# A fused attention and two MLPs on one core: the second MLP's first product by Strassen's algorithm, its second in blocks of 512 columns

## Chip, cores and metric

The kernel runs on one core of one Trainium2 chip. The metric is the device time of one execution in microseconds; the median of three runs of the kernel before is 1016.05 us (1014.8 to 1016.28).

## What is computed

Linear attention with an exponential feature map over 4 batches of 8 heads, 576 tokens each, is followed by two MLPs on the 2304 tokens (512 features, 2048 hidden). The change touches the last one only.

```python
def _moe_ref(x, w_in, w_out):          # first MLP
    h = x @ w_in                       # [2304, 512] @ [512, 2048]
    g = h * (1.0 / (1.0 + np.exp(-h)))
    return (g @ w_out).astype(np.float32)

def _moe2_ref(x, w_in, w_out):         # second MLP
    h = np.maximum(x @ w_in, 0.0)
    return (h * h @ w_out).astype(np.float32)
...
    x = _moe_ref(x=x, **moe_kwargs)
    return _moe2_ref(x=x, **moe2_kwargs)
```

## The kernel before

All data lie transposed: features on the 128 partitions, tokens in the columns. Nearly every float32 factor is split into a high part (ACT casts it, `hi_act`, L351) and a low part (DVE subtracts, `lo_on`, L355), and one product of 128 x 128 weights with a block of tokens is three matmuls: low weights by high tokens, high by low, high by high.

The hidden features are 16 chunks of 128. `chunk(L, i, c, key)` does MLP `L`, token block `i`, chunk `c`: `gemm1` (L987) is 4 parts of 128 input features by three matmuls, 12 matmuls into one PSUM bank `h`; ACT and DVE make the gate out of it (L993, L1000 in the first MLP; relu on ACT, L995, and a multiply on DVE, L1004, in the second), ACT and DVE split the gated block into `gh` and `gl` (L351, L355), and `gemm2` (L1032) adds it with 12 matmuls to the four banks `o` of the output features. The first MLP takes 8 blocks of 288 tokens, the second 6 blocks of 384. After chunk 15 the four banks are evacuated by ACT (L1057) and DVE (L1059) and stored (L1062), the first MLP's to `x2d` in DRAM, from which `x2_of` loads and splits the second MLP's input (L1085).

The second MLP's weights are converted from 64-bit numbers during the attention and the first MLP (`w_conv`, four DVE operations of each 128 x 512 piece, L477 to L487), stored to `w2d` in DRAM (L541), and loaded again and split (`w2_load`, L561, and `w_split`) when the first MLP's weights leave their buffers.

The order is set by a planner (`Plan`): each operation has a key (its due time in units of one chunk), an engine and an assumed cost; `Plan.run` plays the program through and writes each engine's instructions in the order in which they came up. On the chip each engine works that list in order and waits by semaphores.

Of the kernel before, what the change touches and what calls it, by code (L numbers as in the profile page):

```python
# [279 lines left out]
def attention_then_two_mlps(ctx, tc, kT, qT, v, w_phi, w1, w2, out):  # L280
# [264 lines left out]
    stage, staged = [], []  # L545

    def stage_slot():
        if not stage:
            for k in range(2):
                t = wide_pool().tile([128, 3, 512], F32, tag=f"x{k}", name=f"stage{k}")  # L550
                stage.extend(t[:, i] for i in range(3))
        staged.append(stage[len(staged) % len(stage)])
        return staged[-1]

    def w2_load(c, part, key):
        k = ("wf", 1, c, part)
# [640 lines left out]
```

## Time and profile before

| | before |
|---|---|
| median of the runs | 1016.05 us |
| the profiled execution | 1015.75 us |
| its span, first to last instruction | 1013.6 us |
| TensorE (PE) busy | 998.1 us, 98% |
| VectorE (DVE) busy | 603.7 us, 60% |
| ScalarE (ACT) busy | 540.1 us, 53% |
| GpSimd (POOL) busy | 77.2 us, 8% |
| TensorE clock granted, mean | 0.993 |
| DMA, mean | 88 GB/s |

The span holds the instructions; 2.15 us of the execution lie around it. Attention and first MLP share the stretch to some 610 us, the second MLP has the rest. Matmul records overlap, since matmuls are pipelined: how fast they run is read from start to start, in the chain of waits or in the number of records in a window, and not from the mean duration of one.

### The profile page before, as it was taken

Reading aid. Unit: us, or ns where it says so; the run is one execution under the profiler, and the core shown is the slowest. Engines: PE = TensorE matmul, PEld = TensorE weight load, DVE = VectorE, ACT = ScalarE, POOL = GpSimd, SP = SyncE. Lnnn points to the kernel's source line nnn. Section 1 sums busy time; section 2 is a strip of 40 time slices with the busy share of each in tenths; the row PEclk is TensorE's granted clock in tenths of the full one; section 3 lists DMA queues with packets and bytes.
Section 4 is the critical chain, followed back from the end, with each engine's and each line's share of the span. In section 5 each row is a group of like instructions: output and inputs, shape, how many; then the busy total and the mean of one; then the engine's idle time right before and its main releaser. Section 6 shows DMA issues by size and latency. Waiting matters only on the chain.

```text
span 1013.6 us, 17252 instructions
## 1 busy us (share of the span) xinstructions
PE 998.1 (98%) x6656; PEld 971.9 (96%) x6656; DVE 603.7 (60%) x1137; ACT 540.1 (53%) x1295; POOL 77.2 (8%) x56
## 2 busy tenths in 40 slices
PE   9969999999999999999999999999999999999998
PEld 6739999999999999999999999999999999999998
DVE  5989997765656876888986786232232232322322
ACT  6867866776777776877753564232232222322222
POOL 3140003210012200021110000000000000000000
PEclk9979999999999999999999999999999999999999
DMA  8536601131112232544555864010010010100000
GB/s 263 183 112 213 216 25 39 58 86 49 38 32 58 66 113 79 183 131 141 148 137 170 288 219 140 14 51 14 1 63 1 8 55 1 48 1 1 32 1 32
DMA packets 46940, 88.88 MB, mean 88 GB/s; under 512 B 12426, under 2 KB 22794, under 8 KB 44810
## 3 DMA queue, kind: packets, MB, share of 16 engines
q1 hardware_dynamic: 46858, 87.78, 27.6%
q8 instruction: 52, 0.85, 0.3%
q14 instruction: 30, 0.25, 0.1%
HBM read 69.76 MB, written 17.92 MB: 86 GB/s over the span
## 4 chain that ended last, share of the span: by engine, by line
PE 96%; DVE 3%; issue 0%; ACT 0%; POOL 0%
PE h L987 40%; PE o L1032 40%; PE pn L911 5%; PE pk L652 3%; PE pkv L714 3%; PE pkv L760 3%; DVE w L355 1%; PE pq L848 1%; PE pq L849 1%; DVE wc L487 0%; PE pq L846 0%; POOL qm L859 0%; PE warm L439 0%; DVE wc L483 0%; DVE wc L477 0%
## 5 line engine op out<-in xcount | busy, mean ns | idle before, releaser
L1032 PE MATMUL o<-gh,w 128*128 128x288 f32 (+1 forms) x1792 | 442.8, 313 | 0.0
L1032 PEld LDWEIGHTS o<-gh,w 128*128 128x128 f32 x1792 | 313.0, 188 | 2.8 <-issue 2.1
L1032 PE MATMUL o<-gl,w 128*128 128x288 f32 (+1 forms) x896 | 278.7, 311 | 0.0
L987 PE MATMUL h<-x,w 128*128 128x288 f32 x1536 | 224.8, 295 | 0.1
L987 PE MATMUL h<-xw,w 128*128 128x384 f32 x1152 | 215.0, 334 | 0.0
L987 PEld LDWEIGHTS h<-x,w 128*128 128x128 f32 x1536 | 210.9, 188 | 1.0 <-ACT mx L674 0.4
L987 PEld LDWEIGHTS h<-xw,w 128*128 128x128 f32 x1152 | 201.0, 188 | 0.0
L1004 DVE TENSOR_TENSOR a<-h,a 128x384 f32<-128x384 f32 x96 | 53.5, 558 | 216.2 <-ACT a L995 216.0
L995 ACT ACTIVATE a<-h 128x384 f32<-128x384 f32 x96 | 47.2, 492 | 227.9 <-PE h L987 227.9
L1032 PEld LDWEIGHTS o<-gl,w 128*128 128x128 f32 x896 | 168.4, 188 | 0.2
L355 DVE TENSOR_TENSOR gl<-a,gh 128x288 fp32r<-128x288 f32 (+1 forms) x224 | 115.1, 514 | 63.6 <-ACT gh L351 61.3
L351 ACT CAST gh<-a 128x288 fp32r<-128x288 f32 (+1 forms) x224 | 105.3, 470 | 73.3 <-DVE a L1004 54.9
L859 POOL PARTITION_ALL_REDUCE qm<-qp x32 | 73.9, 2326 | 262.1 <-ACT qp L852 230.0
L993 ACT ACTIVATE a<-h 128x288 f32<-128x288 f32 x128 | 52.8, 412 | 74.3 <-PE h L987 73.4
L1000 DVE SCALAR_TENSOR_TENSOR a<-a,h 128x288 f32<-128x288 f32 x128 | 57.6, 450 | 46.9 <-ACT a L993 45.1
L686 ACT ACTIVATE ke<-pk,mx 128x128 f32<-128x128 f32 (+1 forms) x160 | 44.9, 375 | 0.0
L877 ACT ACTIVATE qe<-qp 128x576 f32<-128x576 f32 x64 | 41.8, 681 | 5.6 <-DVE qp L865 5.5
L657 DVE TENSOR_REDUCE mx<-pk 128x4 f32<-128x512 f32 (+1 forms) x48 | 28.5, 596 | 22.6 <-PE pk L652 22.3
L911 PE MATMUL pn<-qh,kv 128*65 128x288 f32 x192 | 41.8, 294 | 0.0
L760 PEld LDWEIGHTS pkv<-v,kp 128*128 128x128 f32 (+1 forms) x320 | 37.0, 191 | 2.2 <-issue 0.8
L760 PE MATMUL pkv<-v,kp 128*128 128x128 f32 (+1 forms) x320 | 38.9, 278 | 0.0
L355 DVE TENSOR_TENSOR qo<-qe,qh 128x576 fp32r<-128x576 f32 x48 | 35.9, 750 | 2.9 <-ACT qh L351 2.3
(90 smaller groups left out, 1027.9 us busy)
## 6 DMA issues: line engine op xcount, KB each, us to landing
wbits<-w SPq DMA_DIRECT2D x16, 1024.0 KB, 5.5
wr<-w SPq DMA_DIRECT2D x32, 512.0 KB, 4.3
w2d<-wc SPq DMA_DIRECT2D x32, 256.0 KB, 3.4
stage<-w2d SPq DMA_DIRECT2D x32, 256.0 KB, 3.9
qr<-qT SPq DMA_DIRECT2D x56, 144.0 KB, 3.3
v<-v SPq DMA_DIRECT2D x16, 325.0 KB, 4.2
kr<-kT SPq DMA_DIRECT2D x16, 288.0 KB, 3.6
qb<-rd SPq DMA_DIRECT2D x32, 144.0 KB, 3.1
```

The costliest lines, as they stand in the source:

```text
L351: nc.scalar.copy(out=dst, in_=src)
L355: e.tensor_tensor(out=dst, in0=src, in1=hi.bitcast(F32), op=ALU.subtract)
L686: nc.scalar.activation(out=get(e)[:nt, a, s], in_=get(ps)[:nt, x * F:(x + 1) * F], func=AF.Exp, scale=1.0 - 2.0 * s, bias=get(mx)[:nt, s, ...
L760: nc.tensor.matmul(get(ps)[:, o:o + 128], get(kps[2 * g + s])[:nt, 2 * i + a], get(vt)[:nt, c:c + 128], start=t == 0 and a == 0 and s == 0 ...
L859: nc.gpsimd.partition_all_reduce(get(mx), get(pr).rearrange("p a t -> p (a t)"), 128, bass.bass_isa.ReduceOp.absmax)
L911: nc.tensor.matmul(get(ps)[:D1, :HB], w, get(e)[:, t], start=x == 0, stop=x == len(ops) - 1)
L987: nc.tensor.matmul(get(ps)[:, :cols], a, x[:, cc], start=k == 0, stop=k == 3 * ND - 1)
L993: nc.scalar.activation(out=a, in_=get(ps)[:, :cols], func=AF.Tanh, scale=0.5)
L995: nc.scalar.activation(out=a, in_=get(ps)[:, :cols], func=AF.Relu)
L1000: nc.vector.scalar_tensor_tensor(out=a, in0=a, scalar=1.0, in1=get(ps)[:, :cols], op0=ALU.add, op1=ALU.mult)
L1004: nc.vector.tensor_tensor(out=a, in0=get(ps)[:, :cols], in1=a, op=ALU.mult)
L1032: nc.tensor.matmul(get(acc)[:, :cols], a, g, start=c == 0 and x == 0, stop=c == NC - 1 and x == 2)
```

## The change

The second MLP runs in two stages instead of one loop.

**First product, by Strassen's algorithm in Winograd's form.** `quad(s, q)` takes 256 hidden features (two chunks) and 576 tokens (`s` = 0 to 3, `q` = 0 to 7). The weights are a 2 x 2 matrix of 256 x 256 blocks, the input one of 256 features by 288 tokens. Instead of eight block products it makes seven, each 2 feature parts by 3 matmuls of 288 columns, 6 matmuls. `w_sums(q)` loads the weight blocks from `w2d` and makes four sums and seven splits once; `x_sums(s)` loads 576 tokens of `x2d`, makes four differences (on DVE for `s` = 0, on POOL after that) and seven splits into the buffers `xt` (seven in all). The results are put together in three PSUM banks: `pa` takes products 1 and 2, `pb` 6, 5 and 3, `pc` 7 and 4. Between two products of one bank another engine reads it: ACT copies product 1 out (`v`, the tile `aq`), DVE makes `u2` = product 6 + `v` (tile `ghq`), `u4` = 6 + 5 + `v` (tile `glq`), and then the four gated blocks `g11`, `g12`, `g21`, `g22`: five additions, one multiply and one square on DVE and six operations on ACT for each quad. The gated blocks go to `gd` in DRAM, 144 KB each.

**Second product.** `gate_of` loads two chunks of a block from `gd` (512 KB), splits them into `xt` buffers, and `down` adds them with 12 matmuls each to four banks, in 4 blocks of 512 tokens and one of 256. Its weights are loaded and split by `w_out` late in the first product.

**Planner.** The second MLP's conversion keys change: all input halves come first, then all output halves.

```diff
-N2 = 384
-NB2 = NTOK // N2
+NS, NQ = NTOK // S, NC // 2
+BLOCKS = [(512 * i, min(512, NTOK - 512 * i)) for i in range(-(-NTOK // 512))]
...
-    "qs": 0.24, "k1": 34.92, "k": 26.62, "ks": 0.3, "qe": 3.1, "w2a": 53.29, "w2b": 3.18, "bx": 3, "pe": 49.5,
+    "qs": 0.24, "k1": 34.92, "k": 26.62, "ks": 0.3, "qe": 3.1, "w2a": 53.0, "w2b": 1.6, "bx": 3, "pe": 49.5,
...
+    def w_sums(q, key):
...
+        SPLITS = ((0, 2, 0), (3, 4, 2), (0, 4, 3))
...
+        def sums():
+            add(3, 2, 3, ALU.add)
+            add(2, 0, 2, ALU.subtract)
+            add(0, 3, 0, ALU.subtract)
+            add(1, 1, 0, ALU.subtract)
...
+    def x_sums(s, key):
...
+        add(t1, b12, b11, first + after(1), "t1")
+        add(t3, b22, b12, first + [(X, "t1")], "t3")
+        add(t2, b22, t1, [(X, "t1"), (X, "t3")] + after(3), "t2")
+        add(t4, b21, t2, [(X, "t2")] + after(2), "t4")
...
+    def quad(s, q, key):
...
+        product(1, pa, True, False)
+        act_op(act(HB, True), lambda: nc.scalar.copy(out=v(), in_=get(pa)[:, :HB]), [(Q, "p1")], [(Q, "v")], [pa, tmp])
+        product(6, pb, True, False)
+        product(2, pa, False, True, [(Q, "v")])
+        product(7, pc, True, False)
+        plus(u2, pb, v, [(Q, "p6"), (Q, "v")], [(Q, "u2")], [])
+        product(5, pb, False, False, [(Q, "u2")])
+        plus(u4, pb, v, [(Q, "p5"), (Q, "v")], [(Q, "u4")], [])
+        plus(gt["22"], pc, u4, [(Q, "p7"), (Q, "u4")], [(Q, "c22")], [g["22"]])
+        product(3, pb, False, True, [(Q, "u4")])
+        product(4, pc, False, True, [(Q, "c22")])
+        plus(gt["12"], pb, v, [(Q, "p3"), (Q, "v")], [(Q, "c12")], [g["12"]])
+        plus(gt["21"], pc, u2, [(Q, "p4"), (Q, "u2")], [(Q, "c21")], [g["21"]])
...
+    def down(i, c, b, r, key):
...
+                for x, (a, y) in enumerate(((1, 0), (0, 1), (0, 0))):
+                    nc.tensor.matmul(
+                        get(acc)[:, :cols], ww[:, c % 2 * 2 + a, f], g[:, y, :cols], start=c == 0 and x == 0,
+                        stop=c == NC - 1 and x == 2,
+                    )
```

**PE, the second MLP.** Of the kernel before, one chunk: `h1_4_15` is the bank of MLP 1 (the second), block 4, chunk 15, `xw0` and `xw1` the block's high and low input, and `o1_4_0` the first output bank with the gated chunk 13.

```order
L987 MATMUL h1_4_15_10891<-xw1_4_9854,w1_15_8299 128x384
L987 MATMUL h1_4_15_10891<-xw0_4_9853,w1_15_8299 128x384
L1032 MATMUL o1_4_0_10485<-gh1_4_13_10845,w1_13_8242 128x384
L1032 MATMUL o1_4_0_10485<-gl1_4_13_10846,w1_13_8242 128x384
L1032 MATMUL o1_4_0_10485<-gh1_4_13_10845,w1_13_8242 128x384
```

Of the changed kernel, the first matmul of each product around quad 4 of `s` = 1 (each product has six): `pb1_4` is bank `pb` of that quad, `xt1_6` the split input of product 6.

```order
L1191 MATMUL pa1_4_9097<-xt1_1_8726,w1_9_8196 128x288
...
L1191 MATMUL pb1_4_9108<-xt1_6_8809,w1_9_8196 128x288
...
L1191 MATMUL pb1_3_9039<-xt1_3_8762,w1_7_8052 128x288
...
L1191 MATMUL pc1_3_9077<-xt1_4_8859,w1_7_8052 128x288
...
L1191 MATMUL pa1_4_9097<-xt1_2_8751,w1_9_8196 128x288
...
L1191 MATMUL pc1_4_9146<-xt1_7_8841,w1_9_8196 128x288
...
L1191 MATMUL pb1_4_9108<-xt1_5_8775,w1_9_8196 128x288
...
L1191 MATMUL pa1_5_9166<-xt1_1_8726,w1_11_8343 128x288
```

Gating and second product no longer stand between the chunks; instead a quad's products 3 and 4 have moved behind the next quad's products 1 and 6, so that two other products lie between product 5 and product 3 of one bank.

**DVE, the start of the second MLP.** Of the kernel before, the rows around the gate of chunk 1 of block 0 (`a1_1_1` names MLP 1 and the chunk's tile; `w1_` tiles are weights).

```order
L477 TENSOR_SCALAR wc1_15_1_8183<-wc1_15_1_8183 128x512
L1004 TENSOR_TENSOR a1_0_0_8190<-h1_0_0_8162,a1_0_0_8190 128x384
L479 TENSOR_SCALAR wc1_15_1_8183<-wc1_15_1_8183 128x512
L355 TENSOR_TENSOR w1_11_8151<-stage1_7499,w1_11_8151 128x512
L1059 TENSOR_SCALAR y0_7_1_8221<-o0_7_1_7595 128x288
L355 TENSOR_TENSOR gl1_0_0_8192<-a1_0_0_8190,gh1_0_0_8191 128x384
L483 SCALAR_TENSOR_TENSOR wc1_15_1_8183<-wr1_15_1_8007,wc1_15_1_8183 128x512
L355 TENSOR_TENSOR w1_12_8179<-stage0_7498,w1_12_8179 128x512
L487 SCALAR_TENSOR_TENSOR wc1_15_1_8183<-wr1_15_1_8007,wc1_15_1_8183 128x512
L355 TENSOR_TENSOR w1_12_8179<-stage0_7498,w1_12_8179 128x512
L355 TENSOR_TENSOR w1_13_8242<-stage0_7498,w1_13_8242 128x512
```

Of the changed kernel, the rows from `u2` of quad 0 of `s` = 0 on (`ghq0_0`), while the last weights are still converted (`wc1_14_1`) and the next quads' weights are split and summed (`w1_9`, `ws4`).

```order
L1206 TENSOR_TENSOR ghq0_0_8177<-pb0_0_8166,aq0_0_8176 128x288
L484 TENSOR_SCALAR wc1_14_1_8104<-wc1_14_1_8104 128x512
L360 TENSOR_TENSOR w1_9_8196<-ws4_8086,w1_8_8151 128x512
L488 SCALAR_TENSOR_TENSOR wc1_14_1_8104<-wr1_14_1_8026,wc1_14_1_8104 128x512
L1230 TENSOR_TENSOR g110_0_8205<-pa0_0_8157,g110_0_8205 128x288
L1206 TENSOR_TENSOR glq0_0_8178<-pb0_0_8166,aq0_0_8176 128x288
L492 SCALAR_TENSOR_TENSOR wc1_14_1_8104<-wr1_14_1_8026,wc1_14_1_8104 128x512
L1206 TENSOR_TENSOR g220_0_8223<-pc0_0_8181,glq0_0_8178 128x288
L360 TENSOR_TENSOR w1_9_8196<-ws4_8086,w1_8_8151 128x256
L1238 SCALAR_TENSOR_TENSOR g220_0_8223<-g220_0_8223 128x288
L1206 TENSOR_TENSOR g120_0_8240<-pb0_0_8166,aq0_0_8176 128x288
L578 TENSOR_TENSOR ws4_8086<-ws4_8086 128x256 x4
```

Where two gate operations a chunk stood among conversions and splits, seven a quad now stand among the same conversions and longer splits, with four sums of 256 columns in each `w_sums`; the first product's own results (`u2`, `u4`) queue behind them.

## Rows read from the trace of the kernel before

**Rows 1.** Windows: microseconds, busy (x instructions) by engine, granted clock, DMA.

```profile
572.00:608.00 36.00, 36.00 (x272) 36.00 (x271) 31.74 (x64) 25.15 (x56) 0.00 (x0) 1.00 0.72 236
...
700.00:1000.00 300.00, 300.00 (x1732) 300.00 (x1732) 89.74 (x164) 81.09 (x165) 0.00 (x0) 1.00 0.05 18
```

**Rows 2.** Chain of waits in order of time: start, length in us, engine, line, instructions.

```profile
392.88 0.71 PE pk L652 x6
...
572.42 3.19 PE h L987 x24
...
607.49 2.11 PE h L987 x12
...
616.96 2.08 PE o L1032 x12
...
1003.84 6.26 PE o L1032 x36
```

**Rows 3.** PE's groups by line and shape: count, busy us, mean ns, idle before.

```profile
L987 PE MATMUL h<-xw,w 128*128 128x384 f32 x1152 | 215.0, 334 | 0.0
...
L1032 PE MATMUL o<-gl,w 128*128 128x384 f32 x384 | 128.3, 334 | 0.0
```

**Rows 4.** DVE's and ACT's groups by line and shape, the same columns.

```profile
L1000 DVE SCALAR_TENSOR_TENSOR a<-a,h 128x288 f32<-128x288 f32 x128 | 57.6, 450 | 46.9 <-ACT a L993 45.1
...
L355 DVE TENSOR_TENSOR qo<-qe,qh 128x576 fp32r<-128x576 f32 x48 | 35.9, 750 | 2.9 <-ACT qh L351 2.3
...
L355 DVE TENSOR_TENSOR w<-stage,w 128x512 fp32r<-128x512 f32 x32 | 21.4, 686 | 0.0
...
L355 DVE TENSOR_TENSOR w<-wc,w 128x1024 fp32r<-128x1024 f32 x16 | 20.4, 1273 | 0.4 <-ACT w L351 0.4
...
L479 DVE TENSOR_SCALAR wc<-wc 128x512 int32<-128x512 int32 x32 | 13.7, 430 | 0.5
...
L663 DVE TENSOR_TENSOR kd<-pk,mx 64x256 f32<-64x256 f32 x3 | 1.2, 407 | 0.0
...
L993 ACT ACTIVATE a<-h 128x288 f32<-128x288 f32 x128 | 52.8, 412 | 74.3 <-PE h L987 73.4
```

**Rows 5.** DVE's timeline, 560 to 575 us: start, length, instruction, idle before it.

```profile
560.29 0.69 DVE L483 SCALAR_TENSOR_TENSOR wc<-wr,wc 128x512 int32<-128x512 int32 x1
561.01 0.69 DVE L487 SCALAR_TENSOR_TENSOR wc<-wr,wc 128x512 int32<-128x512 int32 x1
...
572.22 0.46 DVE L1000 SCALAR_TENSOR_TENSOR a<-a,h 128x288 f32<-128x288 f32 x1 [0.76 <-ACT a L993]
572.59 0.45 DVE L355 TENSOR_TENSOR gl<-a,gh 128x288 fp32r<-128x288 f32 x1
```

**Rows 6.** Timeline of the end, 1001 us on: start, length, instruction.

```profile
1001.59 2.24 PE L987 MATMUL h<-xw,w 128*128 128x384 f32 x12
...
1003.93 0.49 ACT L995 ACTIVATE a<-h 128x384 f32<-128x384 f32 x1 [2.53 <-PE h L987]
...
1009.74 0.34 PE L1032 MATMUL o<-gh,w 128*128 128x384 f32 x1
1010.12 0.56 DVE L1059 TENSOR_SCALAR y<-o 128x384 f32<-128x384 f32 x1 [0.49 <-PE o L1032]
```

**Rows 7.** DVE's timeline: a conversion that waits for ACT, which waits for a DMA.

```profile
568.64 0.43 DVE L477 TENSOR_SCALAR wc<-wc 128x512 f32<-128x512 f32 x1 [2.09 <-ACT wc L471]
```

**Rows 8.** DMA issues by tile: count, KB each, median us to landing; then a window.

```profile
wr<-w SPq DMA_DIRECT2D x32, 512.0 KB, 4.3
...
x2d<-y SPq DMA_DIRECT2D x32, 144.0 KB, 1.8
...
560.00:570.00 10.00, 10.00 (x77) 10.00 (x76) 7.15 (x17) 3.71 (x9) 0.00 (x0) 1.00 0.98 349
```

**Rows 9.** POOL's costliest group.

```profile
L859 POOL PARTITION_ALL_REDUCE qm<-qp x32 | 73.9, 2326 | 262.1 <-ACT qp L852 230.0 <-DVE gl L355 12.2 <-DVE wc L479 11.8
```

**Rows 10.** A window of the attention in which PE waits.

```profile
55.00:60.00 5.00, 2.26 (x5) 1.20 (x6) 4.85 (x5) 2.21 (x5) 5.00 (x4) 0.50 0.02 1
```

More of the change, by code (lines that the diff above doesn't have):

```diff
@@ L543, in w2_store @@
         op(key, "SP", dma(256), store, r=[k], w=[(k, "d")], bufs=[f], unit=u)
[L545 to L556, printed above, removed]
+    SLOT = {1: 0, 2: 1, 4: 2, 6: 3, 3: 4, 7: 5, 5: 6}
@@ new lines, in w_out, with load, hi, lo @@
+    def w_out(c, key):
+        k = ("wf", 1, c, 1)
+        u = plan.unit()
+        f = Buf("c", lambda: cp.tile([128, 512], F32, tag="c", name=f"wo{c}"), None)
+        w = w_tile(2, c // 2)
+        def load():
+            nc.sync.dma_start(out=get(f), in_=w2d[c, :, 512:])
+        def hi():
+            hi_act(get(w)[:, c % 2 * 2], get(f))
+        def lo():
+            lo_on("DVE", get(w)[:, c % 2 * 2 + 1], get(f), get(w)[:, c % 2 * 2])
+        op(key - 2, "SP", dma(256), load, r=[(k, "d"), (("q", NS - 1, max(c // 4 - 1, 0)), "p1")], w=[k], bufs=[f])
+        op(key, "ACT", act(512), hi, r=[k], w=[(k, "hi")], bufs=[f, w], unit=u)
+        op(key, "DVE", dve(512), lo, r=[k, (k, "hi")], w=[(k, "lo")], bufs=[f, w], unit=u)
@@ L1032, in gemm2 @@
                     nc.tensor.matmul(
[L1033 removed]
+                        get(acc)[:, :HB], a, g, start=c == 0 and x == 0, stop=c == NC - 1 and x == 2
                     )
[L1036 removed]
+            op(key + P["g2"], "PE", 3 * MM, gemm2, r=W + [(C, "gh"), (C, "gl")], w=[("acc", i, d)],
                bufs=[acc, gb, w])
@@ L1077, in x2_of @@
[L1077 to L1095 removed]
+                acc = accs[i, d]
@@ new lines, in chunk, with evac, store @@
+                y = Buf("o", lambda d=d: sp.tile([128, HB], F32, tag="o", name=f"y{i}_{d}"), None)
+                e = "ACT" if d % 2 == 0 else "DVE"
+                def evac(d=d, y=y, acc=acc):
+                    if d % 2 == 0:
+                        nc.scalar.mul(out=get(y), in_=get(acc)[:, :HB], mul=0.5)
+                    else:
+                        nc.vector.tensor_scalar_mul(get(y), get(acc)[:, :HB], 0.5)
+                def store(d=d, y=y):
+                    nc.sync.dma_start(out=x2d[:, d, i * HB:(i + 1) * HB], in_=get(y))
@@ new lines, in gate_of, with load, hi, lo @@
+    def gate_of(i, c, key):
+        at, cols = BLOCKS[i]
+        n = f"{i}_{c}"
+        raw = Buf("raw", lambda: rp.tile([128, 2, 512], F32, tag="raw", name="gr" + n), None)
+        of = [("gd", s, c // 2, x) for s in range(at // S, (at + cols - 1) // S + 1) for x in ("11", "12", "21", "22")]
+        of += [(("xr", NS - 1), "lo", prod) for prod in SLOT]
+        def load():
+            nc.sync.dma_start(out=get(raw)[:, :, :cols], in_=gd[:, c:c + 2, at:at + cols])
+        G = ("g2", i, c)
+        op(key - 4, "SP", dma(cols), load, r=of, w=[G], bufs=[raw])
+        for a in range(2):
+            b = Buf("xt", lambda a=a: wide_pool().tile([128, 2, 512], F32R, tag="xt", bufs=NXT, name=f"g2{n}_{a}"), None)
+            def hi(a=a, b=b):
+                hi_act(get(b)[:, 0, :cols], get(raw)[:, a, :cols])
+            def lo(a=a, b=b):
+                lo_on("DVE", get(b)[:, 1, :cols], get(raw)[:, a, :cols], get(b)[:, 0, :cols])
+            op(key, "ACT", act(cols), hi, r=[G], w=[(G, "hi", a)], bufs=[raw, b])
+            op(key, "DVE", dve(cols), lo, r=[G, (G, "hi", a)], w=[(G, "lo", a)], bufs=[raw, b])
+            down(i, c + a, b, [(G, "lo", a)], key + a * cols / HB / 2)
```

327 lines of the change are left out of this document (220 added, 107 removed).

## Prediction

> **What bounds the kernel now.** I read the windows first, then the chain of waits, then PE's groups. In the window from 700 to 1000 us PE is busy 300.00 of 300 us at clock 1.00, while DVE is busy 90 and ACT 81 [rows 1]; the chain runs through PE alone, gate and output products by turns [rows 2]. So the second MLP lasts as long as its matmuls, and a change is worth what it takes off PE's queue, less what PE then waits for.
>
> How long a matmul is comes from start to start: 1732 in 300 us, or 2.08 us for 12, are 0.1733 us each at 384 columns [rows 1, 2]; 24 in 3.19 us are 0.1329 us at 288 columns [rows 2]; 6 in 0.71 us are 0.118 us at 256 [rows 2]. PE reaches the second MLP at 607.49 us and issues its last matmul at 1009.74 us [rows 2, 6]. Its 1152 gate and 3 x 384 output matmuls [rows 3] make 2304 x 0.1733 = 399.3 us; with 24 matmuls of the first MLP that still stand among them (3.2 us) that fills the 402.4 us between. There is no wait in it to gain.
>
> The shorter stage before it matters too: from 572 to 608 us DVE is busy 31.74 of 36 us, 88%, and PE still 36.00 of 36 [rows 1]. A DVE this full does not hold PE up as long as the work comes in time.
>
> **Removed and added matmuls.** The first product: 4 token groups x 8 quads x 7 products x 6 = 1344 matmuls of 288 columns, 1344 x 0.1329 = 178.6 us, in place of 1152 x 0.1733 = 199.6 us: -21.0 us. (At equal blocks Strassen alone would give 1536 - 1344 = 192 matmuls, 25.5 us; 4.5 of them go back for narrower columns.)
>
> The second product: 4 blocks x 192 matmuls of 512 columns and 192 of 256, in place of 1152 of 384. No row has 512 columns. From 288 to 384 columns a matmul grows by 0.421 ns a column, from 256 to 384 by 0.432; 128 more columns on 0.1733 give 0.227 us, which I take. The ends: growth in proportion to columns, 0.231 (+3.1 us in all), and a growth that falls off to 0.36 ns a column, 0.2194 (-5.8 us). So 768 x 0.227 + 192 x 0.118 = 174.3 + 22.7 = 197.0 us for 199.6: -2.6 us. Together -23.6 us.
>
> The Trainium skill ("TensorE: Matmul & The Clock Gate", Back-to-back issue gap) gives columns / 2.4 GHz + 2.5 ns, 162.5 ns at 384, where the row has 173.3. The row decides; by the rule 2304 x 0.1625 = 374.4 us would turn into 1344 x 0.1225 + 768 x 0.2158 + 192 x 0.1092 = 351.3 us, 23.1 us less, so the rule moves each price and hardly the difference.
>
> **What PE waits for inside a quad.** All stands on the order of PE's list. Product 3 needs `u4`, which DVE makes after product 5 of the same bank; two products (12 x 0.1329 = 1.59 us) stand between them. ACT starts 0.1 us after the last matmul it waits for (1001.59 + 2.24 to 1003.93 us [rows 6]), and a 288-column addition takes 0.45 us [rows 4]: `u4` is there after 0.6 us, with 1 us to spare. The other links have more: product 2 waits for ACT's copy (0.41 us [rows 4]) behind three products, product 5 for `u2` behind four, product 4 for `g22`'s sum behind three. Seven DVE operations of 0.45 us are 3.2 us of a quad's 42 x 0.1329 = 5.58 us, six of ACT's of 0.41 are 2.5 us. So `s` = 1 to 3 cost no wait. At a change of `s` DVE has seven splits of 576 columns more, 7 x 0.75 = 5.3 us [rows 4]; a split's buffer is free only when the old product has run in quad 7, but five to seven products (4 to 5.6 us) lie between that and the new one, against ACT 0.7 + DVE 0.75. I put 0.2 us on each of three changes.
>
> POOL's four differences a group have no row. The nearest is a reduction of 2.33 us over 576 columns [rows 9]; four of them, 9.3 us, have eight quads, 45 us, of cover: nothing, and nothing would come of it below a 4-fold price.
>
> **`s` = 0 is the tight place.** Between `u2` of quad 0 and `u2` of quad 7 DVE's list has 83 operations: 47 of 288 columns (0.45 us), 20 sums or splits of 256 (0.41), 8 of 512 (0.69), 3 cheap ones of 512 (0.43), 4 splits of 1024 (1.27) and one of 576 (0.75) [rows 4], 42 us in full lengths. PE has 306 matmuls there, 40.7 us. But independent operations start before their predecessor has ended: 572.22 + 0.46 against 572.59, 0.09 us gained, while a dependent one starts 0.03 us after (560.29 + 0.69 against 561.01) [rows 5]. With some 33 dependent ones DVE needs 35 + 33 x 0.115 = 39 us, 96% of PE's time; in the first two quads it falls up to 2.5 us behind, which is about what lies between `u2` and product 5 there (2.4 to 3.2 us). The bounds: no wait, and every excess as a wait, about 8 us (below). I take 1.
>
> The handover adds one link: the last weight piece (512 KB, 4.3 us to landing [rows 8]) is issued behind four loads of `x2d`, when the DMA engines may be as full as 0.98 [rows 8]; ACT's conversion waits for it, and in ACT's list `v` of quad 1 stands behind that. The same wait was 2.09 us once before [rows 7], then with nothing behind it. I take 0.7 us, 0 to 4.
>
> **Covered.** The stores to `gd` (144 KB, 1.8 us [rows 8]) are four a quad, 105 GB/s; their buffers turn over in over two quads, 11 us. A gate load of 512 KB (4.3 us) has three buffers and seven split ones ahead of a consumption of 24 x 0.227 = 5.4 us a pair, and ACT and DVE need 1.3 us a pair. The tail's evacuation shrinks from 384 to 256 columns (0.56 to 0.41 us): -0.2 us, with the smaller store. The first MLP's list on PE is the same but for a few projections and sums that change places; its DVE list is refilled (conversions reordered, eleven 576-column operations and four `w_sums` more), 43 of 51 us in its last block, less than the 88% above: 0 +- 1 us.
>
> **Sum.** -23.6 - 0.2 + 0.6 + 1 + 0.7 = -21.5 us. The profiled execution's 1015.75 us become 994.2 (span 1013.6 to 992.1, the 2.15 us around it unchanged); the median lies 0.3 us above that execution, so 994.5, and I forecast 994.
>
> **The rivals.**
> 1. *DVE and ACT hold up the handover and `s` = 0.* For: 39 of 40.7 us leaves no room, and every hi-lo pair waits for the other engine. Against: 88% before without loss, and PE's list already puts two or three quads side by side there. If each of eight quads waits 1 us and the weight load 2 to 4: 6 to 13 us in place of 1.7, 998 to 1006, middle 1001.
> 2. *`u4` comes late in every quad.* One mechanism: DVE reaches `u4` after product 3 is due, in all 32 quads. It starts to cost when `u4` lies over 1.6 us after product 5, and eats the whole gain when PE waits 21.8 / 32 = 0.68 us a quad, `u4` then 2.3 us late. For: DVE's list is strict, and three operations or a split of 576 in front of `u4` are 1.4 to 2 us. Against: in the list of `s` = 1 only one gate multiply stands directly ahead of it, and DVE has 40% to spare. At 1.2 us a quad: 994 + 38 = 1032. If such waits let the clock fall, more: where PE was busy 2.26 of 5 us the granted clock was 0.50, the lower level of 1.2 GHz [rows 10]. The Trainium skill (the same page, A second HAM failure mode) warns of just this form, short waits between groups that go round PSUM banks. The trace before shows no such fall after 100 us, and no run here goes round banks in this way.
> 3. *512 columns cost less than the line says,* or several of the wait terms turn out as gains: 768 x 7.6 ns = 5.8 us less, and no waits: 986.
> 4. *Half of rival 2:* 0.6 us a quad, the gain gone, 1013 to 1017.
>
> **Chances.** Forecast (990 to 998): 0.70. Rival 1: 0.18. Rival 3: 0.04. Rival 4: 0.02. Rival 2: 0.06. The range from 990 to 1004 holds the forecast and most of rival 1, some 0.8; 990 is no wait with 0.225 us at 512 columns. A measurement of this kernel tells 0.2%, 2 us, from no change: faster 0.92, the same 0.02, slower 0.06.
>
> **What would show it.** Right: 1344 matmuls of 288 columns at 0.133 us from start to start, in the chain one product on the next; 0.227 at 512 columns; PE busy and clock 1.00 through all of the second MLP; DVE some 95% busy for 40 us after the handover and below 65% afterwards. Wrong: idle time of PE put down to `u4` or `u2` on DVE (rivals 1 and 2, told apart by whether it ends with `s` = 0), a granted clock below 1, a 512-column step other than 0.227, PE idle before the first output product, or a first MLP that ends later than 607 us.

## The result, and the profile after

The changed kernel takes 1003.87 us (median; 1002.71 to 1004.59), the kernel before 1015.79 us in the same comparison: a ratio of 0.9883, 95% interval 0.9866 to 0.9900. It is 11.9 us faster. The forecast was 994; 1003.87 is the upper edge of the range, where rival 1 lay.

| | before | after |
|---|---|---|
| median | 1015.79 us | 1003.87 us |
| the profiled execution, its span | 1015.75, 1013.6 us | 1002.71, 1000.9 us |
| the second MLP begins | 607.49 us | 611.18 us |
| its first product ends, by the chain | interleaved | 798.26 us |
| its last matmul ends, about | 1010.1 us | 997.4 us |
| PE, DVE, ACT, POOL busy | 98, 60, 53, 8% | 98, 68, 58, 9% |

The chain of waits of the changed kernel at the seams (start, length in us, engine, tile, line, instructions); it answers to [rows 2]:

```profile
608.00 1.60 PE h L1035 x12
609.59 1.59 PE o L1071 x12
611.18 0.80 PE pa L1191 x6
611.98 0.81 PE pb L1191 x6
...
797.47 0.80 PE pc L1191 x6
798.26 199.16 PE y L1294 x951
```

The whole second product but its first nine matmuls is one piece of the chain: no load from `gd`, no split and no evacuation holds PE up there. The windows of the changed kernel (us, busy and count by engine in the order PE, weight loads, DVE, ACT, POOL, then granted clock, DMA share, GB/s) answer to [rows 1]:

```profile
480.00:520.00 40.00, 37.35 (x269) 36.64 (x268) 34.54 (x68) 26.59 (x61) 9.15 (x4) 0.96 0.54 153
...
612.00:652.00 40.00, 38.88 (x282) 37.54 (x282) 38.05 (x80) 21.03 (x47) 6.46 (x4) 1.00 0.49 170
...
640.00:790.00 150.00, 150.00 (x1127) 150.00 (x1126) 106.24 (x229) 84.29 (x195) 11.63 (x8) 1.00 0.46 153
...
800.00:960.00 160.00, 160.00 (x690) 129.77 (x689) 47.27 (x70) 41.70 (x70) 0.00 (x0) 1.00 0.41 124
```

From 640 to 790 us PE is busy throughout and runs 1127 matmuls of 288 columns, 0.133 us each: the first product does what was forecast. From 800 to 960 us it runs 690 of 512 columns, 160 / 690 = 0.232 us each, where I had put 0.227 (and 0.231 as the upper end); from the starts of the single matmuls it is 0.2324. And there are two stretches in which PE waits: at 500 us, in the first MLP, and in the first 40 us of the second. All of PE's waits from 480 us on are named by these groups (engine, tile, line, releaser: total us, times, longest):

```profile
PE pn L963 <- DVE qo L360: 2.6, 2, 2.3
...
PE pb L1191 <- DVE glq L1206: 0.6, 1, 0.6
PE pa L1191 <- ACT aq L1213: 0.4, 1, 0.4
```

Put beside the sum of the prediction (span 992.1 us, measured 1000.9, so 8.8 us short):

| term | predicted | measured | difference |
|---|---|---|---|
| first MLP and attention, start of the second MLP | 0 | 611.18 - 607.49 = +3.7 | +3.7 |
| first product's matmuls | 178.6 | 1344 x 0.1332 = 179.0 | +0.4 |
| waits and slow restarts in the first product | 1 + 0.7 + 0.6 = 2.3 | 187.1 (611.18 to 798.26) - 179.0 - 24 of the first MLP 3.2 - 9 of the second product 2.1 = 2.8 | +0.5 |
| second product's matmuls | 197.0 | 199.16 + 2.1 = 201.2 | +4.2 |
| tail | -0.2 | 0.0 | +0.2 |

These make 9.0 us; the rest is rounding. So two terms account for almost all of the miss: a wait in a stage that the change only touches by the order of its conversions, and the price of a wide matmul. (The first row is a balance: at 470 us the changed kernel's trace is 0.6 us ahead of the kernel before; the loss at 500 us itself is 4.6 us.)

### The profile page after: what moved, and what is told of

It reads as the page before. It is cut to its first block, busy times and chain, and to the rows that moved or that the text cites. A ratio compares the mean times of both kernels' runs of the same rounds, so it can differ in the third digit from the quotient of the medians.

```text
span 1000.9 us, 17956 instructions
## 1 busy us (share of the span) xinstructions
PE 981.7 (98%) x6656; PEld 920.4 (92%) x6656; DVE 677.7 (68%) x1295; ACT 579.5 (58%) x1385; POOL 94.6 (9%) x68
## 4 chain that ended last, share of the span: by engine, by line
PE 93%; DVE 4%; DMA 1%; issue 1%; ACT 0%; POOL 0%; SPq 0%; DVEq 0%
PE h L1035 20%; PE y L1294 20%; PE o L1071 19%; PE pb L1191 7%; PE pc L1191 5%; PE pa L1191 5%; PE pn L963 5%; PE pk L704 3%; PE pkv L766 3%; PE pkv L812 3%; DVE w L360 1%; PE pq L900 1%; PE pq L901 1%; DVE wc L492 1%; DVE wc L488 1%
## 5 line engine op out<-in xcount | busy, mean ns | idle before, releaser
L1071 PE MATMUL o<-gh,w 128*128 128x288 f32 x1024 | 232.1, 298 | 0.0
L1294 PE MATMUL y<-g,w 128*128 128x512 f32 (+1 forms) x960 | 201.7, 372 | 0.0
L1294 PEld LDWEIGHTS y<-g,w 128*128 128x128 f32 x960 | 167.5, 188 | 33.6
L1071 PEld LDWEIGHTS o<-gh,w 128*128 128x128 f32 x1024 | 172.7, 188 | 2.6 <-issue 1.9
L1071 PE MATMUL o<-gl,w 128*128 128x288 f32 x512 | 150.4, 294 | 0.0
L360 DVE TENSOR_TENSOR g<-gr,g 128x512 fp32r<-128x512 f32 (+1 forms) x80 | 51.0, 638 | 130.3 <-ACT g L356 130.2
L1071 PEld LDWEIGHTS o<-gl,w 128*128 128x128 f32 x512 | 96.4, 188 | 0.2
L1191 PE MATMUL pb<-xt,w 128*128 128x288 f32 x576 | 88.4, 296 | 0.7 <-DVE glq L1206 0.6
L1191 PEld LDWEIGHTS pb<-xt,w 128*128 128x128 f32 x576 | 80.6, 188 | 1.4 <-DVE glq L1206 0.8
L360 DVE TENSOR_TENSOR gl<-a,gh 128x288 fp32r<-128x288 f32 x128 | 64.2, 502 | 11.8 <-ACT gh L356 10.8
L1191 PE MATMUL pc<-xt,w 128*128 128x288 f32 x384 | 61.1, 295 | 0.0
```

Of the source, the lines that this page charges most:

```text
L360: e.tensor_tensor(out=dst, in0=src, in1=hi.bitcast(F32), op=ALU.subtract)
L1071: nc.tensor.matmul(get(acc)[:, :HB], a, g, start=c == 0 and x == 0, stop=c == NC - 1 and x == 2)
L1191: nc.tensor.matmul(get(ps)[:, :HB], wpart(a, prod)[:, f], x[:, y, cc], start=first and k == 0, stop=k == 5, skip_group_check=True,)
L1294: nc.tensor.matmul(get(acc)[:, :cols], ww[:, c % 2 * 2 + a, f], g[:, y, :cols], start=c == 0 and x == 0, stop=c == NC - 1 and x == 2,)
```

## The wait in the first MLP

What stands at 500 us of the changed kernel. DVE's timeline (start, length, line, operation, tiles; in brackets the idle time before it and what ended it):

```profile
500.32 0.45 DVE L360 TENSOR_TENSOR x<-x,x 128x288 fp32r<-128x288 f32 x1
501.65 0.92 DVE L1001 TENSOR_TENSOR x<-qn,qb 64x288 f32<-64x288 f32 x2 [0.88 <-DMA qb<-rd]
502.60 0.76 DVE L360 TENSOR_TENSOR qo<-qe,qh 128x576 fp32r<-128x576 f32 x1
```

PE's timeline:

```profile
503.41 0.50 PE L963 MATMUL pn<-qo,kv 128*65 128x288 f32 x1 [2.28 <-DVE qo L360]
```

and the windows at and after this wait:

```profile
502.00:504.00 2.00, 0.59 (x3) 0.57 (x4) 1.92 (x4) 1.09 (x3) 0.00 (x0) 0.81 0.92 311
504.00:506.00 2.00, 2.00 (x10) 1.94 (x9) 1.87 (x5) 0.98 (x3) 0.00 (x0) 0.50 0.54 172
506.00:508.00 2.00, 2.00 (x15) 2.00 (x14) 1.90 (x4) 1.00 (x3) 0.00 (x0) 0.83 0.25 79
508.00:510.00 2.00, 2.00 (x17) 2.00 (x17) 1.94 (x3) 1.01 (x3) 1.19 (x1) 1.00 0.82 235
```

DVE's multiplies for `x` (attention's scaling) wait 0.88 us for a DMA; the split `qo` stands behind them in DVE's list; and PE waits for `qo`. After that the granted clock falls to 0.50, the lower level of 1.2 GHz, and between 504 and 506 us the window counts 10 matmuls, 17 once the clock is back (508 to 510 us). The cost is more than the waits of 2.6 us: between 480 and 520 us PE ran 269 matmuls, 304 in the kernel before, 35 x 0.133 = 4.7 us. The same window of the kernel before, and of `late_diffs` (below), which has the changed kernel's lists up to here:

```profile
480.00:520.00 40.00, 40.00 (x304) 40.00 (x303) 36.24 (x78) 27.08 (x63) 8.82 (x4) 1.00 0.49 127
...
480.00:520.00 40.00, 36.61 (x273) 35.85 (x272) 34.99 (x69) 26.76 (x61) 9.10 (x4) 1.00 0.56 153
```

All eight other kernels with the same lists up to here (below: `late_diffs`, `diffs_on_dve`, `mixed_blocks`, `blocks_480`, `blocks_384`, `u4_two_more`, `u4_four_more`, `eighth_product`) show waits of PE for `qo` of 1.9 to 2.4 us in this place, and six of them 1.2 to 1.4 us for `ql` besides; they lose 4.0 to 4.9 us of matmuls there, as the changed kernel does. So it belongs to the list. Neither the DMA nor the clock is needed for it. In `late_diffs` the multiplies follow on their predecessor without a wait for the DMA, and the clock stays at 1.00 (it fell in `diffs_on_dve` and `blocks_480` alone); DVE, PE and POOL there:

```profile
499.97 0.75 DVE L360 TENSOR_TENSOR qo<-qe,qh 128x576 fp32r<-128x576 f32 x1
500.63 0.45 DVE L360 TENSOR_TENSOR x<-x,x 128x288 fp32r<-128x288 f32 x1
501.13 0.92 DVE L1001 TENSOR_TENSOR x<-qn,qb 64x288 f32<-64x288 f32 x2
502.08 0.76 DVE L360 TENSOR_TENSOR qo<-qe,qh 128x576 fp32r<-128x576 f32 x1
...
507.80 1.74 DVE L360 TENSOR_TENSOR ql<-qr,ql 64x576 fp32r<-64x576 f32 x1
...
502.89 0.35 PE L963 MATMUL pn<-qo,kv 128*65 128x288 f32 x1 [1.52 <-DVE qo L360]
...
509.59 0.40 PE L900 MATMUL pq<-ql,wst_lo 128*128 128x288 f32 x1 [1.20 <-DVE ql L360]
...
507.19 6.84 POOL L911 PARTITION_ALL_REDUCE qm<-qp  x3 [12.35 <-ACT qp L904]
```

What all nine share in their traces (no run moved these operations alone) is that three operations which PE does not need yet, a split of `x` and the two multiplies, 1.4 us together, stand between two `qo` that PE needs one after the other. The DMA and the clock only change how the loss comes about: where the clock stays up, PE waits a second time, for a `ql` that comes late because DVE was held up beside a reduction on POOL (here the split `ql` itself takes 1.74 us, 0.76 elsewhere; the next section has this effect).

The first MLP's list on PE is nearly that of before; DVE's was refilled because the conversions of the weights got new due times. Two kernels change these alone.

**The due times of before** (`keys_of_before`):

```diff
-    "qs": 0.24, "k1": 34.92, "k": 26.62, "ks": 0.3, "qe": 3.1, "w2a": 53.0, "w2b": 1.6, "bx": 3, "pe": 49.5,
+    "qs": 0.24, "k1": 34.92, "k": 26.62, "ks": 0.3, "qe": 3.1, "w2a": 53.29, "w2b": 3.18, "bx": 3, "pe": 49.5,
...
-            at = base2 - W2A + W2B * (c if part == 0 else NC + c)
+            at = base2 - W2A + W2B * c
```

> Edit: the conversions of the second MLP's weights get the due times of the kernel before (input and output half of a chunk side by side, 3.18 units a chunk from 53.29 units ahead) in place of all input halves first, 1.6 units apart from 53.0 ahead. Nothing else. In the changed kernel PE's first product begins 3.7 us later (611.18 us) than the second MLP of before (607.49 us): PE waits 2.3 and 0.4 us at 500 us for qo on DVE, which stands behind an operation that waits 0.88 us for the DMA of qb, and after that the granted clock is 0.50 to 0.83 for some 4 us. Theory A (the new order of the conversions put these together): the first product begins at 607 to 608 us, 1000 to 1000.5. Theory B (it comes from something else in the change): it begins at 610.5 to 611.3 us, 1003 to 1004. In both, the weights of quads 6 and 7 come later here and can cost 0 to 2 us at s = 0.

**The first due time alone** (`keys_shifted`): input halves still come first, but all of them 0.29 units earlier.

```diff
-    "qs": 0.24, "k1": 34.92, "k": 26.62, "ks": 0.3, "qe": 3.1, "w2a": 53.0, "w2b": 1.6, "bx": 3, "pe": 49.5,
+    "qs": 0.24, "k1": 34.92, "k": 26.62, "ks": 0.3, "qe": 3.1, "w2a": 53.29, "w2b": 1.6, "bx": 3, "pe": 49.5,
```

> Edit: the conversions' first due time alone, 53.29 units ahead in place of 53.0; input halves still first. Theory A (it is the order, input halves first): PE still waits 2 to 3 us at 500 us, the first product begins at 610.5 to 611.5 us, 1003 to 1004. Theory C (where the waits fall is a matter of small shifts in the planner's order, and this order is one of many): the waits lie elsewhere or are gone, and the first product begins anywhere from 607 to 611 us, 1000 to 1004.

Measured: `keys_of_before` 1002.88 us (ratio to before 0.9883, 0.9866 to 0.9899), `keys_shifted` 998.42 us (0.9833, 0.9819 to 0.9848). The window of `keys_shifted` over the same stretch:

```profile
480.00:520.00 40.00, 40.00 (x304) 40.00 (x303) 36.32 (x79) 28.41 (x64) 7.25 (x4) 1.00 0.51 145
```

and its chain of waits where the second MLP begins:

```profile
607.03 0.80 PE pa L1191 x6
```

304 matmuls, as before, and a start at 607.03 us; the two `qo` follow each other with one operation of 0.45 us between them, and the multiplies come at 505.19 us only. In `keys_of_before` the start is at 607.61 us, but the first product then has waits of 2.0, 1.3 and 1.3 us, so that the time is that of the changed kernel. They come behind later conversions, sums and splits of weights and behind POOL's differences, which stretch three conversions from 0.42, 0.43 and 0.69 to 1.28, 1.28 and 1.68 us; how much is due to either wasn't separated. Putting the input halves first is therefore not what made the wait (theory A falls): a shift of the same order by 0.29 units takes it away. Theory C stands: which of DVE's operations happen to stand ahead of one that PE needs is a matter of small shifts in the planner's order. The shift is worth 5.4 us of the median (1003.87 to 998.42), and 4.2 us at the start of the second MLP in the traces (611.18 to 607.03); the rest is within the spread of the runs. Why the DMA for `x` landed late in some of the nine kernels (DVE waited 0 to 0.88 us for it) stays open.

## POOL's differences hold up DVE

The prediction gave POOL's four differences for the next `s` no price, because they have 45 us of cover. DVE's timeline of the changed kernel just after the start of the second MLP:

```profile
613.26 0.84 DVE L484 TENSOR_SCALAR wc<-wc 128x512 int32<-128x512 int32 x1
614.03 0.68 DVE L360 TENSOR_TENSOR w<-ws,w 128x512 fp32r<-128x512 f32 x1
614.63 1.91 DVE L488 SCALAR_TENSOR_TENSOR wc<-wr,wc 128x512 int32<-128x512 int32 x1
616.47 0.45 DVE L1230 TENSOR_TENSOR g<-pa,g 128x288 f32<-128x288 f32 x1
616.84 0.44 DVE L1206 TENSOR_TENSOR glq<-pb,aq 128x288 f32<-128x288 f32 x1
617.20 1.17 DVE L492 SCALAR_TENSOR_TENSOR wc<-wr,wc 128x512 int32<-128x512 int32 x1
618.29 0.45 DVE L1206 TENSOR_TENSOR g<-pc,glq 128x288 f32<-128x288 f32 x1
618.65 1.28 DVE L360 TENSOR_TENSOR w<-ws,w 128x256 fp32r<-128x256 f32 x1
```

and POOL's:

```profile
612.39 1.44 POOL L1144 TENSOR_TENSOR xs<-xr 128x576 f32<-128x576 f32 x1 [96.69 <-DMA xr<-x2d]
614.54 1.46 POOL L1144 TENSOR_TENSOR xs<-xr,xr 128x576 f32<-128x576 f32 x1 [0.71 <-DMA xr<-x2d]
615.96 3.69 POOL L1144 TENSOR_TENSOR xs<-xr,xs 128x576 f32<-128x576 f32 x2
```

L488 begins 0.1 us after a difference on POOL and ends 0.54 us after it has ended: it waited for it. Four operations take 0.84, 1.91, 1.17 and 1.28 us for 0.43, 0.69, 0.69 and 0.42 elsewhere, 3.0 us more together, all of them with operands in SBUF alone; those that read a PSUM bank (L1206, L1230) keep their 0.45. So `glq` (`u4`) begins at 616.84 and ends at 617.28, and PE waits for it until 617.33. The Trainium skill ("SBUF — State Buffer", Who interferes with whom) states this: GpSimd and VectorE share a pair of ports under an exclusive lock. A VectorE instruction with two SBUF inputs contends with one of GpSimd that reads SBUF, and one in a two-port mode contends with GpSimd so that whichever starts first keeps the other out for its whole instruction. The rows agree for L488, L492 and L360, which have two inputs in SBUF; L484 has one, and whether it ran in a two-port mode no run here shows. I had not weighed that rule.

**Held back to quad 4** (`late_diffs`):

```diff
+        deps += [(("q", 0, 4), "p1")] if s == 1 else []
```

> Edit: the loads of x_sums(1), and so its four differences on POOL, wait until product 1 of quad 4 of s = 0 has run. Nothing else. In the changed kernel DVE's operations with both operands in SBUF are longer while these differences run (612 to 620 us): 0.84 for 0.43, 1.91 for 0.69, 1.17 for 0.69, 1.28 for 0.42 us, together 3.0 us, and PE loses about 2.8 us between 611 and 640 us. Theory A (the differences on POOL hold DVE): the four operations fall back to 0.43 to 0.69 us, most of the 2.8 us is won, 1001.5 to 1002.5. Theory B (DVE's own list is too long for s = 0, rival 1 of the prediction): the wait stays within 0.5 us, 1003.5 to 1004. In both the differences' new place, quads 4 to 6, has no wait.

**On DVE** (`diffs_on_dve`):

```diff
-            e = "DVE" if s == 0 else "POOL"
+            e = "DVE"
```

> Edit: the four differences of s = 1 to 3 run on DVE like those of s = 0, none on POOL. Theory A (POOL holds DVE): DVE's operations at 612 to 620 us have their own lengths; the differences of s = 1 cost DVE 4 x 0.75 = 3.0 us, but behind the quads' operations; PE's loss at s = 0 falls from 2.8 to 0.5 to 1.5 us, 1001.5 to 1003. Theory B (DVE is full anyway): 3.0 us more work in 96% full time make 1 to 3 us more wait, 1005 to 1007. For s = 2 and 3 no wait in either, since DVE has 40% to spare there.

Measured: `late_diffs` 1001.84 us (0.9866, 0.9850 to 0.9882), `diffs_on_dve` 1002.66 us (0.9874, 0.9859 to 0.9889). Both intervals overlap that of the changed kernel, so the case rests on the traces. In both the operations at 613 us have their own lengths again; DVE's timeline of `late_diffs`:

```profile
612.77 0.42 DVE L484 TENSOR_SCALAR wc<-wc 128x512 int32<-128x512 int32 x1
...
613.71 0.68 DVE L488 SCALAR_TENSOR_TENSOR wc<-wr,wc 128x512 int32<-128x512 int32 x1
...
642.90 1.28 DVE L360 TENSOR_TENSOR w<-ws,w 128x256 fp32r<-128x256 f32 x1
...
645.72 3.02 DVE L578 TENSOR_TENSOR ws<-ws 128x256 f32<-128x256 f32 x4
```

The first loss is gone: between 612 and 640 us PE ran 192 matmuls in the changed kernel and 213 in `late_diffs`:

```profile
612.00:640.00 28.00, 26.88 (x192) 25.54 (x192) 26.82 (x56) 14.20 (x32) 6.46 (x4) 1.00 0.57 194
...
612.00:640.00 28.00, 28.00 (x213) 28.00 (x212) 25.96 (x60) 15.85 (x35) 1.15 (x1) 1.00 0.64 204
```

But POOL now works from 638.85 to 647 us, and there the last split and the last sums of weights grow from 0.42 to 1.28 and from 1.79 to 3.02 us; PE waits 1.3 us for `u4` behind them. Theory A holds for the mechanism; my expectation that quads 4 to 6 had no wait was wrong. In `diffs_on_dve` PE runs 300 matmuls from 612 to 652 us (282 in the changed kernel), but waits 1.6 us for `u4` at 658, 704 and 749 us, the changes of `s`: three microseconds of differences in DVE's list hold `u4` up there by themselves. By its trace it gains nothing in the first product as a whole (187.5 us for 187.1), nor in the span (1000.9 us both).

```profile
PE pb L1191 <- DVE glq L1206: 1.6, 3, 0.6
```

**Both causes together.** `shift_late4` is `keys_shifted` with the differences held back to quad 4, `shift_late6` with quad 6 (and `x_sums(1)` written behind `quad(0, 6)` so that it can wait for it; its due times are the same).

> Edit: the shifted due time of the conversions (53.29 units ahead, which took the wait at 500 us away) and x_sums(1) held back to quad 4 of s = 0 (which won 1.1 us of the 2.65 us that PE loses between 600 and 660 us) together. Theory A (two separate causes): the gains add up, 998.4 - 1.1 = 997.3 us. Theory B (the loss at s = 0 depends on the rest of DVE's list, which the shift changed): 998 to 999.

> Edit: the shifted due time, and x_sums(1) held back to quad 6 of s = 0, where DVE's conversions, sums and splits of weights are nearly over. Theory A (POOL's differences cost PE time only where DVE has SBUF-only work and no room): nearly all of the 2.5 us lost between 600 and 660 us comes back, 996 to 997. Theory B (the differences are then late themselves, since products 6 and 7 of s = 1 need them): the loss moves to the change from s = 0 to 1, 998 to 1001.

Measured: `shift_late4` 999.33 us (0.9834, 0.9819 to 0.9849), no better than `keys_shifted` alone: PE still waits 1.2 us for `u4` and 0.5 us for a sum of `pc` between 620 and 660 us. Here the gains don't add up (theory B), since the differences hit another part of a list that the shift had changed. `shift_late6`: 996.70 us (0.9806, 0.9789 to 0.9822), with no wait of PE after the attention's first 100 us; its window over the stretch that lost 2.5 us above:

```profile
612.00:652.00 40.00, 40.00 (x301) 39.78 (x300) 36.99 (x83) 23.40 (x51) 2.79 (x2) 1.00 0.58 190
```

301 matmuls for 282, 19 x 0.133 = 2.5 us. It is the best kernel here, 7.2 us below the changed kernel by the medians: the first wait (5.4 us) and the differences on POOL (1.7 us; 2.3 us of the first product by the traces) together are what lies between 1003.9 and 996.7.

## What a wide matmul costs

**Five widths in one kernel** (`mixed_blocks`), **480 and 384 columns** (`blocks_480`), **384 alone** (`blocks_384`):

```diff
-BLOCKS = [(512 * i, min(512, NTOK - 512 * i)) for i in range(-(-NTOK // 512))]
+BLOCKS = [(0, 508), (508, 496), (1004, 480), (1484, 448), (1932, 372)]      # mixed_blocks
+BLOCKS = [(0, 480), (480, 480), (960, 480), (1440, 480), (1920, 384)]       # blocks_480
+BLOCKS = [(0, 384), (384, 384), (768, 384), (1152, 384), (1536, 384), (1920, 384)]   # blocks_384
```

> Edit: the second product's blocks are 508, 496, 480, 448 and 372 columns in place of 512 four times and 256. The trace gives the time from start to start for each. Rows so far: 256 columns 0.118, 288 0.1332, 384 0.1733 us, each 11 to 13 ns above columns / 2.4 per ns, and 512 0.2319 us, 18.6 ns above. Theory A (only a full 512 is dear): 508 0.225, 496 0.220, 480 0.2133, 448 0.200, 372 0.168 us. Theory B (the surplus grows steadily with the columns from 384 on): 508 0.230, 496 0.2246, 480 0.2173, 448 0.2026, 372 0.168 us. By A the stage is 192 x 1.026 = 197.0 us, by B 199.4, against 200.7 in the changed kernel.

> Edit: the second product's blocks are 480 columns four times and 384 in place of 512 four times and 256. By theory A (only a full 512 is dear): 768 x 0.2133 + 192 x 0.1733 = 197.1 us for 200.7, -3.6, and +0.15 for the longer last evacuation: 1000.4. By theory B (the surplus grows steadily from 384 on): 768 x 0.2173 + 33.3 = 200.2, -0.5 + 0.15: 1003.5.

> Edit: the second product in six blocks of 384 columns, as wide as in the kernel before, in place of 512 four times and 256. By 0.176 us a matmul, as 384 columns took in this stage in the run with blocks of 480 and 384: 1152 x 0.176 = 202.8 us for 201.1 in the changed kernel, +1.7 and +0.15 for the last evacuation. By 0.1733 us, as in the kernel before: 199.6 us, -1.5 + 0.15. It tells whether the second product's part of the change gained anything.

Measured from start to start, in us:

| columns | 256 | 372 | 384 | 448 | 480 | 496 | 508 | 512 |
|---|---|---|---|---|---|---|---|---|
| second product | 0.1186 | 0.170 | 0.176 | 0.204 | 0.2178 and 0.220 | 0.2265 | 0.2288 | 0.2324 |
| kernel before | 0.118 | | 0.1733 | | | | | |
| above columns / 2.4 per ns, ns | 12 | 15 | 16 (13) | 17 | 18 and 20 | 20 | 17 | 19 |

Only theory B is near: there is nothing special about 512, and what a matmul takes above its columns grows from 12 to nearly 20 ns. The surplus does not grow evenly (17 ns at 508, 20 at 496). The stage took the same in the three divisions into five blocks: 951 of the 960 matmuls 199.16 us (512 and 256), 199.10 (480 and 384) and 199.44 (mixed). The times are 1001.91 us for `blocks_480` (0.9869, 0.9854 to 0.9884; its interval overlaps that of the changed kernel), 1002.48 for `mixed_blocks` and 1004.87 for `blocks_384`, the last two of one run each, so that the stage's own length decides. The window of `blocks_384` that answers to the one of 512 columns above:

```profile
800.00:960.00 160.00, 160.00 (x911) 160.00 (x910) 49.69 (x90) 45.87 (x91) 0.00 (x0) 1.00 0.43 126
```

160 us for some 910 matmuls, 0.176 us each; 1152 of them are 202.8 us. So the wider blocks did gain, 202.8 - 201.2 = 1.6 us, but the stage as a whole lost 1.6 us against before (199.6), because the same 384 columns take 0.176 us here and took 0.1733 there. The prediction's -2.6 us for the second product was +1.6. Half of the 5.4 ns missing at 512 columns is the starting point, 0.176 us here for 0.1733, which did not carry over to the new loop; the other half is the step from there, 0.0564 us for 128 columns (0.441 ns a column) where I had put 0.0537. Within the new loop a line through its own 256 and 384 columns gives 0.2334 for 512, 1 ns too much: the line itself held. The upper bound, growth in proportion to the columns from 0.1733 us, was passed (0.231). Why the same width takes 1.5% longer in this loop stays open: the single distances repeat every five matmuls (174 to 181 ns) or seven (228 to 241 ns at 512), which does not divide the loop's twelve, while before they were 173 to 174 throughout. The DMA share is higher here, 0.41 from 800 to 960 us for 0.07 in the kernel before, but at 288 columns the first product has the 0.133 us of before beside a share of 0.46.

The Trainium skill ("TensorE: Matmul & The Clock Gate", Back-to-back issue gap) has 2.5 ns above the columns for every width; it calls this the gap of an isolated matmul and gives about 131 ns at 512 columns for a sustained stream of weight loads and matmuls. The runs show 12 to 20 ns above the columns and 232 ns at 512, so neither figure fits this stream. What the prediction drew from it, that the rule moves each price and hardly the difference, was off by 4 us: 23.1 us less by the rule, 399.3 - 179.0 - 201.2 = 19.1 by the runs.

## The room inside a quad

The prediction put `u4` 1 us ahead of its need and made its lateness the slower rival. Two kernels make it late on purpose, by writing the same sum more than once for `s` = 1 to 3:

```diff
-        plus(u4, pb, v, [(Q, "p5"), (Q, "v")], [(Q, "u4")], [])
+        plus(u4, pb, v, [(Q, "p5"), (Q, "v")], [(Q, "u4")], [], 3 if s else 1)    # u4_four_more: 5
...
-                nc.vector.tensor_tensor(out=out(), in0=get(ps)[:, :HB], in1=y(), op=ALU.add)
+                for _ in range(times):
+                    nc.vector.tensor_tensor(out=out(), in0=get(ps)[:, :HB], in1=y(), op=ALU.add)
```

> Edit: for s = 1 to 3 the addition that makes u4 is done three times over into the same buffer, so u4 comes 2 x 0.37 = 0.75 to 0.9 us later and the order of all else is the same. The prediction put u4 0.6 us after product 5 and product 3 1.59 us after it, 1 us to spare. Theory A: within 0.5 us of the changed kernel, no wait of PE for u4 in s = 1 to 3. Theory B (no room there, rival 2 of the prediction): 24 quads x 0.75 us = 18 us more.

> Edit: as before with five additions in place of one, u4 1.5 to 1.8 us later. Theory A (1.59 us between product 5 and product 3, 1 us to spare): u4 lies 0.5 to 0.8 us behind, 24 x 0.5 to 0.8 = 12 to 19 us more, 1016 to 1023, as much as the whole gain; PE waits in each quad of s = 1 to 3 for u4. Theory B (more room than thought, since PE's list lies ahead of the due order): under 5 us more.

Measured: 1011.35 and 1036.36 us (one run each), 7.5 and 32.5 us more than the changed kernel. The timeline of `u4_four_more` in a regular quad, of DVE and of PE:

```profile
757.50 2.43 DVE L1207 TENSOR_TENSOR glq<-pb,aq 128x288 f32<-128x288 f32 x5
...
759.99 1.06 PE L1191 MATMUL pb<-xt,w 128*128 128x288 f32 x6 [0.92 <-DVE glq L1207]
```

and PE's wait for `u4` from 660 to 840 us:

```profile
PE pb L1191 <- DVE glq L1207: 26.0, 24, 1.8
```

Five additions into one buffer take 2.43 us, 0.49 us from one to the next (not the 0.37 of independent ones), so `u4` comes 1.97 us late and PE waits 0.92: 1.05 us were to spare, as forecast. With two more, 0.98 us, the quads stand just at the edge: a regular one loses about 0.2 us in slow restarts, and where splits of 576 columns or POOL's differences stand beside the quad, at the changes of `s`, PE waits up to 1.57 us. The two changes from `s` = 1 to 2 and from 2 to 3 make up 4.7 of the 8.8 us by which its quads of `s` = 1 to 3 are longer in the trace: my expectation of under 0.5 us was wrong, and the prediction's 0.2 us for each change of `s` (none was measured in the changed kernel) would have been right only with less room. In `u4_four_more` a quad lasts 6.78 us (753.21 to 759.99) for 5.60, so a recorded wait of 0.92 us costs 1.2. Of the 0.26 us between, 0.10 is a slow restart (six matmuls behind a wait take 1.06 us, 0.96 elsewhere); the other 0.16 is the record, whose wait begins at a matmul's end, 0.29 us after its start, when the next would have started after 0.13. Rival 2's price, one for one, was too low, and its point of decision was 1 us away.

The granted clock tells the other half of that rival. Through the stretch with these waits it stays at the upper level; windows of `u4_four_more`:

```profile
700.00:760.00 60.00, 50.31 (x363) 48.20 (x361) 46.10 (x102) 24.68 (x60) 5.73 (x4) 1.00 0.32 107
```

The form of which the Trainium skill warns ("TensorE: Matmul & The Clock Gate", A second HAM failure mode), short waits between groups that go round PSUM banks, did not bring the clock down here, with 24 waits of 0.9 to 1.8 us. The waits of the first MLP at 500 us did so in three of nine kernels (the longest wait 2.3, 1.6 and 1.4 us) and not in the other six (1.5 to 1.8 us); a wait of 2.0 us in the first product of `keys_of_before` left it at 1.00 as well. So the length of a wait alone does not tell, and what does stays open.

## What the eighth product would have cost

`eighth_product` makes product 7 of every quad twice, so that PE has the matmuls of the plain algorithm beside Strassen's additions:

```diff
-                for cc in range(2):
+                for cc in range(2) if prod != 7 else (0, 1, 0, 1):
+                    k = k % 6
```

> Edit: product 7 of every quad is made twice (12 matmuls in place of 6, the second pass starts the bank anew), so that there are eight products' matmuls as in the plain algorithm, with the same additions, loads and stores. 192 matmuls x 0.1332 us = 25.6 us. Theory A (PE alone bounds the first product): 25 to 25.6 us more for s = 1 to 3, and at s = 0, with 6.4 us more of PE time, the loss of 2.65 us shrinks: 1003.9 + 23 to 25.6 = 1027 to 1029.5. Theory B (other engines share the bound of the first product): less than 20 us more.

Measured: 1028.3 us (one run), 24.4 more. 192 more matmuls are 25.6 us, and the loss in the first product shrinks by 0.8 us in the trace (2.8 to 2.0). Theory A holds: PE bounds the first product, and the seventh-for-eighth saving is worth 24 to 26 us. Against the kernel before it is 20.6 us, since 288 columns are dearer for each column than 384.

## Why the prediction was right or wrong

- **What bounds the kernel: right.** PE is busy through 640 to 790 us and through the second product; the time is the number of matmuls by their distances, plus waits that can be counted.
- **First product, -21.0 us: right** (-20.6).
- **Second product, -2.6 us: wrong, +1.6.** The mis-sized term is the distance at 512 columns, 0.227 forecast and 0.232 measured. The step that failed is the starting point, a price from a loop of another form (0.1733 us at 384 columns, 0.176 in this one), and for the other half the slope taken from there.
- **Waits inside a quad: right in size.** 1.05 us to spare for `u4` against 1 forecast; no wait in `s` = 1 to 3, not even at the changes of `s`.
- **`s` = 0 and the handover: 1.7 us forecast (2.3 with the changes of `s`), 2.8 measured.** DVE was 38.05 of 40 us busy from 612 to 652 us, 95%, as forecast, but the agreement of both numbers is luck: the cause was another one. 3.0 us of DVE's 38.05 are waiting for POOL, without these differences the first three quads take 2.7 us less (`late_diffs`), and the step that failed is "POOL's four differences ... nothing": their cover was right and their side effect was left out. The kernel before has a weak sign of it: an operation of `rr` (L929) takes 0.91 us at 513.78 us, inside a reduction on POOL, and 0.16 at its median; but two conversions with two SBUF inputs beside the same reduction keep their 0.69 and 0.65 us. Once these differences are out of the way, a DVE at 92 to 93% costs PE nothing there (36.99 of 40 us in `shift_late6`, 301 matmuls; 37.12 in `diffs_on_dve`, 300): rival 1, that a DVE so full holds up `s` = 0 by itself, isn't borne out. The wait for the last weight piece, 0.7 us forecast, I can't find as such: the one wait for ACT's `v` is 0.4 us.
- **The first MLP, 0 +- 1 us: wrong, +3.7.** I counted DVE's work in the refilled list (43 of 51 us) and called it less than the 88% of before, but a wait does not come from the sum. It comes from what stands in DVE's list ahead of a split that PE needs: 1.4 us of other work between two `qo`, and in the changed kernel 0.88 us of waiting for a DMA on top.
- **Covered: right.** Stores to `gd`, loads from it and the evacuation cost nothing; the tail is unchanged, where -0.2 us was forecast.
- **After `s` = 0 DVE is 69% busy** (92.83 of 134 us from 656 to 790 us), not below 65%. Probably each operation counts there with its full 0.45 us, since it starts after a gap and not beside its predecessor; no run tests this.

The time lay in the range because of its reach to rival 1, whose 998 to 1006 was for another mechanism. Of the forecast's own 990 to 998 the changed kernel missed 6 us; with the wait in the first MLP and POOL's interference removed, `shift_late6` lies in it at 996.70 us, while the wide matmul's 4.2 us stay.

## What to carry to other kernels

Saving matmuls pays in full where PE is the bound, but price a wider matmul from runs of that loop: the line from 256 to 384 columns held at 512, its starting point from another loop did not. When work goes to GpSimd, ask not only whether it has cover but which of VectorE's SBUF-only operations run beside it, and put it where VectorE has room. And when a scheduler refills a list, look for what stands ahead of each operation that PE needs next, not at the sum of the work: here a shift of one due time by 0.29 of a chunk was worth 5.4 us, beside 11.9 for the whole change.
